# Layer one in pairs of chunks with 7 of 8 sub-products from the third pair, and an issue order reckoned at build time

## The chip, the cores and the metric

The kernel runs on one core of a Trainium2 chip. The metric is device time in microseconds (us). TensorE (PE) multiplies, VectorE (DVE), ScalarE (ACT) and GpSimd (POOL) work on tiles, and SyncE (SP) issues the DMAs. Every engine takes its own instructions in the order in which the program issued them.

## The reference

```python
def _attn_ref(q, k, v, centroids):            # B=2, H=8, S=768, D=64, 16 clusters
    ...
    mask = q_assign[:, :, :, None] == k_assign[:, :, None, :]
    scores = np.where(mask, scale * np.matmul(q, k.transpose(0, 1, 3, 2)), -1000000000.0)
    ...
    return np.matmul(attn, v)

def _moe_ref(x, w_in, w_out):                 # layer one: x 1536 x 512, w_in 512 x 2048 (float64)
    h = x @ w_in
    g = np.where(h > 0.0, h, np.exp(np.minimum(h, 0.0)) - 1.0)
    return g @ w_out

def _moe2_ref(x, domain_probs, w1, w2):       # layer two: 4 experts, 512 -> 1024 -> 512
    p = domain_probs / (domain_probs.sum(-1, keepdims=True) + 1e-09)
    for e in range(4):
        h = np.maximum(x @ w1[e], 0.0)
        out += p[:, e:e + 1] * (h @ w2[e])
    return out
```

## The kernel before

Attention (lines 100 to 587) runs first and leaves its output transposed in `xT`: three blocks of 512 tokens, each value as a high part and a low part, which together hold it to more bits than one float32r operand. A product of two split operands takes three matmuls: high by high, high by low, low by high. The change leaves the order of attention as it is.

Layer one cuts the 2048 hidden features into 16 chunks of 128. `emit_G1` (L783) forms one chunk for one block of 512 tokens: 4 slices of the features times 3 matmuls of 128x512, 12 in all, into one of two PSUM tiles `h`. The ELU follows: ACT takes Relu and Exp (L798, L799), DVE combines them with the PSUM value (L800), POOL splits the result into `gh` and `gl` (L801, L802). `emit_G2` (L968) multiplies with the chunk's rows of w_out: 4 outputs of 3 matmuls (L989). The chunks are taken in groups of 2, 4, 5 and 5 (`SIZES`, L598), a group being run for the first block, then the second, then the third; the four outputs stay in PSUM over all chunks of the group and are then copied to (L1012, ACT) or added to (L1014, DVE) the accumulators `acc`.

The weights of layer one arrive as float64. `w_split` (L716) converts a chunk from the 64-bit pattern in passes of 128x1024: ACT (L735), DVE (L737, L740, L743), ACT (L741, L747), DVE (L749), then ACT makes the high part (L751) and POOL the low part (L754). The first two chunks are converted during attention.

Layer two takes 16 pairs of chunks (256 features). A pair's first product is a 2 by 2 block product with 7 sub-products in place of 8 (`product`, L806, 6 matmuls each): for tokens 0 to 1023 with 512 columns (42 matmuls), for the last 512 tokens with 256 columns (42 matmuls). It needs sums of the operands: of the weights `w2_split` (L680, DVE), of x `x2_first`, `x2_second`, `x2_last` (L895 to L964). `quad_early` (L816) and `quad_late` (L838) issue the sub-products; three times TensorE goes on adding to a PSUM tile after ACT has copied it away:

```python
product(px, A11, "B11", s, True, True)
act.activation(out=m1, in_=px, func=AF.Copy)
product(pz, S1, "T1", s, True, True)
product(px, S2, "T2", s, False, True)
act.activation(out=u2, in_=px, func=AF.Copy)
```

The second product has 12 outputs of 6 matmuls (L989), which DVE scales by the expert's share and adds to `acc` (L1003).

The order is fixed at build time by hand: `tick` (L1060) and `advance` (L1056) move the weight and x generators on by one step at a time between the matmul steps, at positions given by `start` and `load_at` (L1041 to L1053). SP issues a chunk's two loads (`w_load`, L644) in that order too.

Of the kernel before, what the change touches and what calls it, by code (L numbers as in the profile page):

```python
# [46 lines left out]
def kernel(  # L47
# [37 lines left out]
    xT = [[xp.tile([128, 2, 512], F32R, tag=f"x{tb}{kk}", name="xT") for kk in range(KD)] for tb in range(NB)]  # L85
# [14 lines left out]
    def attention():  # L100
# [379 lines left out]
        def do_XS(w, i):  # L480
            j, r, hi, lo, cs = x_rows(w)
            if r == 0:
                return
            b, hp = divmod(j, HP)
            tb, o = divmod(b * S + cs.start, 512)
            hi, lo = (xT[tb][hp][:, i, o:o + XW] for i in range(2))
            pool.tensor_scalar(hi, xs_t[j][:, cs], 1.0, 0.0, ALU.mult, ALU.add)
            pool.tensor_tensor(lo, xs_t[j][:, cs], hi.bitcast(F32), ALU.subtract)  # L488
# [10 lines left out]
        def weights(n):  # L499

            for i in range(2):
                raw = cv_p.tile([128, 512, 2], I32, tag="raw", name="w_raw")
                w_load(n, [raw], i)
                yield
                yield
                tmp = cv_p.tile([128, 2, 512], I32, tag="tmp", name="w_tmp")
                yield from w_split(n, [tmp[:, x] for x in range(2)], i)
# [81 lines left out]

    SIZES = [2, 4, 5, DFF // 128 - 11]  # L598
    NSLOT = 9
    groups, chunks, steps = [], [], []  # L600
    at = 0
    for i, n in enumerate(SIZES):
        for tb in range(NB):
            for c in range(n):
                steps.append((1, tb, len(chunks) + c, c == 0, c == n - 1, i == 0, i == len(SIZES) - 1))
        for c in range(n):
            chunks.append((1, at + c))
        at += n
    NC1 = len(chunks)
    NP = E * F2 // 256  # L610
    BLOCKS = ((0, 8), (8, 4))
    for i in range(NP):
        for blk in range(len(BLOCKS)):
            steps.append((2, blk, NC1 + i, True, True, i == 0, i == NP - 1))
        chunks.append((2, i))
    NS = len(steps)

    last = [f"{t}{n % NSLOT}" for n in range(NC1 - SIZES[-1], NC1) for t in "hl"]
    early = [f"{t}{n % NSLOT}" for n in range(NC1, NC1 + NSLOT - SIZES[-1]) for t in "hl"]
    W2_TAGS = (early[:3] + early[4:6], last[1:4] + last[5:7])  # L620
    B22_TAG, G_TAG = early[3], last[4]
    A11, A12, A22, S1, S2, S3, S4 = range(7)

    X2_TAGS = (
        dict(zip(
            (A11, A12, S1, S2, S3, A22, S4),
            (("qh", "ql"), ("kl", "x00"), ("x01", "x02"), ("x03", "x10"), ("x11", "x12"), ("x13", early[6]),
             (early[7], last[0])),
        )),
        [f"x2{kk}" for kk in range(KD)] + last[7:],  # L630
    )
    W0 = 2
    LAG = 2
    moe_p = {}
    st_t, w_t = {}, {}

    def home(tag, shape, name, dt=F32R):
        p = xp if tag[0] == "x" else gen if tag[0] in "qk" else w01 if tag[1] in "01" else moe_p["w"]
        return p.tile(shape, dt, tag=tag, name=name)

    def w_tiles(n):
        return [home(f"{t}{n % NSLOT}", [128, 2, 512], f"w{t}{n % NSLOT}") for t in "hl"]

    def w_load(n, raw=None, half=None):  # L644
        ly, f = chunks[n]
# [4 lines left out]
        if ly == 1:  # L650
            for i, a in enumerate(raw):
                if half == 1 or i == 1:
                    src = w_out.bitcast(I32)[f * 128:(f + 1) * 128, :]
                    sp.dma_start(out=a.rearrange("p f t -> p (f t)"), in_=src)
                else:
                    src = w_in.bitcast(I32)[:, f * 256:(f + 1) * 256].rearrange("(k p) f -> p k f", p=128)
# [3 lines left out]
        else:  # L660
            e, f = divmod(f, F2 // 256)
# [9 lines left out]
    def split(h, l, x, eng):  # L671

        act.activation(out=h, in_=x, func=AF.Copy)
        yield
# [4 lines left out]

    def w2_split(n):  # L680

# [5 lines left out]
        t = gen.tile([128, 4, 2, 128], F32, tag="kh", name="T")  # L687
        dve.tensor_tensor(out=t[:, 0], in0=b12, in1=b11, op=ALU.subtract)
        dve.tensor_tensor(out=t[:, 2], in0=b22, in1=b12, op=ALU.subtract)
        yield  # L690
        dve.tensor_tensor(out=t[:, 1], in0=t[:, 0], in1=b22, op=ALU.subtract)
        dve.tensor_tensor(out=t[:, 3], in0=t[:, 1], in1=b21, op=ALU.add)
        yield
        ops = {}
        for x, names in (
            (a[:, :, 0], ("B11", "B21")), (t[:, 0:2].rearrange("p a k f -> p (a k) f"), ("T1", "T2")),
# [7 lines left out]
            else:  # L704
                o = home(tags[len(ops) // 2], [128, 2, m, 128], "w1op")
            yield from split(o[:, 0], o[:, 1], x, dve)
            for i, nm in enumerate(names):
                ops[nm] = [[o[:, z, 2 * i + kk] for kk in range(2)] for z in range(2)]
            yield
        h, l = (home(tag, [128, 2, 512], "w2op") for tag in tags[3:])  # L710
        b = b.rearrange("p (c d) -> p c d", c=2)
        yield from split(h, l, b, dve)
        w_t[n] = ops, (h, l)
        yield

    def w_split(n, tmp=None, half=None):  # L716
        if chunks[n][0] == 2:
            yield from w2_split(n)
            return
        a = st_t.pop(n)  # L720
        if n not in w_t:
            w_t[n] = w_tiles(n)
        h, l = w_t[n]
        if half is not None:
            h, l = h[:, half], l[:, half]

        small = tmp is not None
        a32, sg = tmp if small else [gtile(("qh", "kl", "kh")[n % 3], "wa", [128, 2, 512], I32), gtile("ql", "wsg", [128, 2, 512], I32)]  # L730
        at = (slice(None),) * (len(a.shape) - 1)
        hi, lo = a[at + (1,)], a[at + (0,)]
        x, sg = a32.bitcast(F32), sg.bitcast(F32)

        act.activation(out=x, in_=hi.bitcast(F32), func=AF.Abs)  # L735
        yield
        dve.tensor_scalar(x, x, LOW, TOP, ALU.max, ALU.min)  # L737
        if small:
            yield
        dve.tensor_scalar(a32, a32, 3, 0x40000000, ALU.logical_shift_left, ALU.bitwise_xor)  # L740
        act.activation(out=sg, in_=hi.bitcast(F32), func=AF.Sign)  # L741
        yield
        dve.scalar_tensor_tensor(  # L743
            out=a32, in0=lo, scalar=29, in1=a32, op0=ALU.logical_shift_right, op1=ALU.bitwise_or
        )
        yield
        act.activation(out=x, in_=x, func=AF.Abs)  # L747
        yield
        dve.tensor_tensor(out=x, in0=x, in1=sg, op=ALU.mult)  # L749
        yield  # L750
        act.activation(out=h, in_=x, func=AF.Copy)  # L751
        if small:
            yield
        pool.tensor_tensor(l, x, h.bitcast(F32), ALU.subtract)  # L754
        yield

    def moe():
# [8 lines left out]
        g_t, x2, x2_gen, w_gen2 = {}, [{}, {}], [[], []], {}  # L766
        turn = [0, 0]

# [14 lines left out]
        def emit_G1(s):  # L783
            ly, tb, n = steps[s][:3]
            if ly == 2:
                return
            wh, wl = w_t[n]
            ps = ps_h.tile([128, 512], F32, tag=f"h{s % 2}", name="h")
            for kk in range(KD):
                f = slice(kk * 128, (kk + 1) * 128)  # L790
                xh, xl = xT[tb][kk][:, 0], xT[tb][kk][:, 1]
                for i, (w, x) in enumerate(((wh, xh), (wh, xl), (wl, xh))):
                    pe.matmul(  # L793
                        ps, lhsT=w[:, 0, f], rhs=x, start=(kk == 0 and i == 0), stop=(kk == KD - 1 and i == 2)
                    )
            gh, gl = g_pair(1)
            r, gg = (scratch([128, 512], nm) for nm in ("r", "gg"))
            act.activation(out=r, in_=ps, func=AF.Relu, scale=-1.0)  # L798
            act.activation(out=r, in_=r, func=AF.Exp, scale=-1.0)  # L799
            dve.scalar_tensor_tensor(out=gg, in0=r, scalar=-1.0, in1=ps, op0=ALU.add, op1=ALU.max)  # L800
            pool.tensor_scalar(gh, gg, 1.0, 0.0, ALU.mult, ALU.add)  # L801
            pool.tensor_tensor(gl, gg, gh.bitcast(F32), ALU.subtract)  # L802
            g_t[s] = [(gh, gl)]


        def product(ps, a, b, s, start, stop):  # L806
            blk, n = steps[s][1:3]
            x, w = x2[blk][a], w_t[n][0][b]
# [7 lines left out]
        def quad_early(s):  # L816
            big = steps[s][1] == 0
# [4 lines left out]
            else:  # L822
                m1, u2, u3, c11 = (x[:, i] for x in (scratch([128, 2, n], "u"), scratch([128, 2, n], "u")) for i in range(2))
                c = scratch([128, 2, n], "c")
                c1, c2 = c[:, 0], c[:, 1]
            product(px, A11, "B11", s, True, True)
            act.activation(out=m1, in_=px, func=AF.Copy)  # L827
            product(pz, S1, "T1", s, True, True)
            product(px, S2, "T2", s, False, True)
            act.activation(out=u2, in_=px, func=AF.Copy)  # L830
            product(py, A12, "B21", s, True, True)
            dve.tensor_tensor(out=c11, in0=py, in1=m1, op=ALU.add)
            product(px, S3, "T3", s, False, True)
            act.activation(out=u3, in_=px, func=AF.Copy)
# [237 lines left out]
        def run_all(it):  # L1072
            for _ in it:
                pass
# [100 lines left out]
```

## Time and profile before

| | us |
|---|---|
| runs | 1036.28, 1039.0, 1037.94; median 1037.94 |
| profiled execution | 1037.14, of which the span 1035.3 |
| PE busy | 1016.5 (98% of the span), 5593 matmuls |
| DVE / ACT / POOL busy | 721.0 (70%) / 517.9 (50%) / 392.4 (38%) |

The span goes from the first to the last instruction of one profiled execution; what lies around it makes up the rest of its time. Matmuls overlap, so the pitch of a matmul is read from the chain of waits, where a run of matmuls stands with its time, and not from its own duration.

### The profile page before, as it was taken

Reading aid. Unit: us, or ns where it says so; the run is one execution under the profiler, and the core shown is the slowest. Engines: PE = TensorE matmul, PEld = TensorE weight load, DVE = VectorE, ACT = ScalarE, POOL = GpSimd, SP = SyncE. Lnnn points to the kernel's source line nnn. Section 1 sums busy time; section 2 is a strip of 40 time slices with the busy share of each in tenths; the row PEclk is TensorE's granted clock in tenths of the full one; section 3 lists DMA queues with packets and bytes.
Section 4 is the critical chain, followed back from the end, with each engine's and each line's share of the span. In section 5 each row is a group of like instructions: output and inputs, shape, how many; then the busy total and the mean of one; then the engine's idle time right before and its main releaser. Section 6 shows DMA issues by size and latency. Waiting matters only on the chain.

```text
span 1035.3 us, 14919 instructions
## 1 busy us (share of the span) xinstructions
PE 1016.5 (98%) x5593; PEld 881.6 (85%) x5593; DVE 721.0 (70%) x1151; ACT 517.9 (50%) x1002; POOL 392.4 (38%) x391
## 2 busy tenths in 40 slices
PE   8999999999999999999999999999999999999998
PEld 7989999989877888888887888888888888888887
DVE  7999999898679675233475766665776665776665
ACT  4989999888777554333345232332232323232321
POOL 4888888989688767344452000000000000000000
PEclk9999999999999999999999999999999999999999
DMA  6746654430333222000102101111101111101003
GB/s 157 188 110 157 145 136 111 118 91 3 125 120 123 82 82 82 1 0 1 41 1 82 40 3 41 41 41 41 41 1 41 42 41 41 41 1 41 1 1 122
DMA packets 61463, 66.65 MB, mean 64 GB/s; under 512 B 28944, under 2 KB 47376, under 8 KB 61392
## 3 DMA queue, kind: packets, MB, share of 16 engines
q1 hardware_dynamic: 61392, 65.71, 22.4%
q8 instruction: 44, 0.72, 0.3%
q14 instruction: 27, 0.22, 0.1%
HBM read 43.08 MB, written 3.15 MB: 45 GB/s over the span
## 4 chain that ended last, share of the span: by engine, by line
PE 80%; DVE 8%; POOL 4%; ACT 4%; issue 2%; DMA 1%; SPq 0%; DVEq 0%; POOLq 0%; ACTq 0%
PE a L989 35%; PE h L811 23%; PE h L793 11%; PE x L456 4%; PE tps L423 3%; PE s L375 2%; PE s L378 2%; POOL p L411 2%; DVE pl L444 1%; DVE nm L384 1%; DVE wa L743 1%; PE qkps L199 1%; DVE wa L737 1%; PE lps L244 1%; POOL xT L488 1%
## 5 line engine op out<-in xcount | busy, mean ns | idle before, releaser
L811 PE MATMUL h<-x,w1op 128*128 128x512 f32 (+1 forms) x1344 | 245.0, 337 | 2.2 <-ACT u L827 1.4
L811 PEld LDWEIGHTS h<-x,w1op 128*128 128x128 f32 x1344 | 211.7, 189 | 32.1 <-ACT u L827 1.6
L989 PE MATMUL a<-w2op,gh 128*128 128x512 f32 x768 | 237.2, 390 | 0.0
L989 PEld LDWEIGHTS a<-w2op,gh 128*128 128x128 f32 x768 | 142.1, 188 | 28.6 <-ACT acc L999 0.3
L1003 DVE SCALAR_TENSOR_TENSOR acc<-a,prob,acc 128x512 f32<-128x512 f32 x180 | 134.5, 748 | 34.2 <-PE a L989 34.1
L989 PE MATMUL a<-w2op,gl 128*128 128x512 f32 x384 | 149.6, 390 | 0.0
L793 PE MATMUL h<-xT,wh 128*128 128x512 f32 x384 | 118.6, 390 | 0.6 <-DVE gg L800 0.6
L800 DVE SCALAR_TENSOR_TENSOR gg<-r,h 128x512 f32<-128x512 f32 x48 | 32.9, 685 | 104.2 <-ACT r L799 83.0
L411 POOL TENSOR_SCALAR p<-e,sm 128x768 f32<-128x768 f32 x96 | 89.2, 936 | 34.4 <-DVE sm L405 24.4
L384 DVE TENSOR_REDUCE nm<-s 128x1 f32<-128x768 f32 x96 | 90.9, 947 | 2.8 <-PE s L378 2.6
L393 ACT ACTIVATE e<-s,nm 128x768 f32<-128x768 f32 x96 | 86.6, 902 | 4.3 <-POOL p L411 3.3
L423 PE MATMUL tps<-ident,p 128*128 128x128 f32 x576 | 83.7, 277 | 3.3 <-DVE pl L444 3.1
L793 PEld LDWEIGHTS h<-xT,wh 128*128 128x128 f32 x384 | 71.9, 188 | 16.3 <-DVE gg L800 1.4
L989 PEld LDWEIGHTS a<-w2op,gl 128*128 128x128 f32 x384 | 72.1, 188 | 15.2
L444 DVE TENSOR_TENSOR pl<-tps,ph 128x512 fp32r<-128x512 f32 x112 | 76.2, 684 | 6.6 <-ACT ph L436 5.0
L798 ACT ACTIVATE r<-h 128x512 f32<-128x512 f32 x48 | 28.6, 596 | 100.4 <-PE h L793 100.4
L801 POOL TENSOR_SCALAR gh<-gg 128x512 fp32r<-128x512 f32 x48 | 42.9, 894 | 94.5 <-DVE gg L800 92.6
L456 PE MATMUL x<-ph,v 128*128 128x256 f32 x288 | 76.4, 297 | 0.1
L989 PE MATMUL a<-gh,wh 128*128 128x512 f32 x192 | 74.9, 390 | 1.0 <-ACT acc L1012 0.9
L989 PE MATMUL a<-gl,wh 128*128 128x512 f32 x192 | 74.7, 389 | 0.0
L793 PE MATMUL h<-xT,wl 128*128 128x512 f32 x192 | 74.7, 389 | 0.0
L989 PE MATMUL a<-gh,wl 128*128 128x512 f32 x192 | 74.7, 389 | 0.0
(163 smaller groups left out, 1855.6 us busy)
## 6 DMA issues: line engine op xcount, KB each, us to landing
st<-in_moe_w_dram SPq DMA_DIRECT2D x32, 512.0 KB, 4.3
st<-in_moe_w_in_dram SPq DMA_DIRECT2D x14, 512.0 KB, 3.8
st<-in_moe_w_out_dram SPq DMA_DIRECT2D x14, 512.0 KB, 4.6
QA<-qh SPq DMA_DIRECT2D x30, 192.0 KB, 3.9
nq<-in_q_dram SPq DMA_DIRECT2D x16, 192.0 KB, 3.7
nk<-in_k_dram SPq DMA_DIRECT2D x16, 192.0 KB, 3.8
nv<-in_v_dram SPq DMA_DIRECT2D x8, 384.0 KB, 4.3
QB<-ql SPq DMA_DIRECT2D x16, 192.0 KB, 3.9
```

What stands on the lines that cost most here:

```text
L384: dve.tensor_reduce(out=m_t[w][:, i:i + 1], in_=s_t[HALF * w + i][:, :, 0:384], axis=AX.XY, op=ALU.max, negate=True)
L393: act.activation(out=e, in_=s_t.pop(u)[:, :, 0:384], func=AF.Exp, bias=m_t[w][:, i:i + 1], accum_out=e_t[w][0][:, i:i + 1])
L411: pool.tensor_scalar(p, e_t[w][1 + i].rearrange("p a b -> p (a b)"), e_t[w][0][:, i:i + 1], 1.0, ALU.mult, ALU.mult)
L423: pe.transpose(ps[:, x, :], p_t[w][i][:, c * 128:(c + 1) * 128], ident)
L444: dve.tensor_tensor(out=l, in0=ps, in1=h.bitcast(F32), op=ALU.subtract)
L456: pe.matmul(x_t[w], lhsT=v2[j][:, r, c, :], rhs=t[:, :, c, :], start=(c == 0 and t is ph[w]), stop=(c == T - 1 and t is pl[w]),)
L793: pe.matmul(ps, lhsT=w[:, 0, f], rhs=x, start=(kk == 0 and i == 0), stop=(kk == KD - 1 and i == 2))
L800: dve.scalar_tensor_tensor(out=gg, in0=r, scalar=-1.0, in1=ps, op0=ALU.add, op1=ALU.max)
L801: pool.tensor_scalar(gh, gg, 1.0, 0.0, ALU.mult, ALU.add)
L811: pe.matmul(ps, lhsT=w[wz][kk], rhs=x[xz][:, kk], start=(start and kk + i == 0), stop=(stop and kk == 1 and i == 2), skip_group_check=True,)
L989: pe.matmul(ps, lhsT=x, rhs=y, start=(opens and i == 0), stop=(closes and i == len(ops) - 1))
L1003: dve.scalar_tensor_tensor(out=t, in0=ps, scalar=pr, in1=t, op0=ALU.mult, op1=ALU.add)
```

## The change

Layer one is taken in 8 pairs of chunks. Each pair is run for the first block (a), the second (b) and the third (c). From the third pair on (`NPLAIN = 2`), blocks a and b are formed together by `quad_one`, the same 7 sub-products as in layer two with the ELU behind them; block c keeps `emit_G1`. For this the sums of x are made once (`x1_ops`) and those of the weights for each pair (in `w_pair`). The second product closes its PSUM tiles after each pair (`emit_G2_one`, 6 matmuls for an output). In layer two the first pair uses 8 plain sub-products (`plain_two`); the sums of x come after it (`x2_ops`). The high part of an activation moves from POOL to ACT, and low parts and sums go to DVE or POOL, whichever ends earlier by the reckoned clocks.

The order of the vector work is no longer written out. While the program is built, a clock for each engine is advanced by an assumed price of each instruction, with one more clock (`port`) for work that DVE and POOL can't do at the same time. Work of the weights and sums stands in `back`; `fill` issues it ahead of an instruction of the matmul path if it would end no later than that instruction could start, plus a tolerance. The loads of domain_probs move from the thirteenth step of layer one to its start.

```diff
-    SIZES = [2, 4, 5, DFF // 128 - 11]
-    NSLOT = 9
...
+    NC1 = DFF // 128
+    NP1 = NC1 // 2
+    NPLAIN = 2
+    END, LEAD = 4, 4
+    TIGHT, TOL, LOOSE = 0.0, 0.5, 0.7
...
+    clk, port = {act: 1.0, dve: 1.6, pool: 1.0, pe: 0.0}, [0.0]
+    COST = {act: (0.11, 0.00083), dve: (0.07, 0.00105), pool: (0.2, 0.0021)}
+    LATE, MM, MM2, BIAS = 0.16, 0.227, 0.53, 0.0
...
+    def ends(e, n, ready, lock):
+        if e is None:
+            return min(ends(dve, n, ready, lock) + BIAS, ends(pool, n, ready, lock))
+        return max(clk[e], ready, port[0] if lock else 0.0) + COST[e][0] + COST[e][1] * n
...
+    def w_pair(p):
...
+        yield from both(*(w_convert(n) for n in two))
+        yield from until("G1", p - 2)
+        yield from both(*(w_split(n, 0) for n in two))
...
+            for o, x, y, f in (
+                (b11, b12, b11, ALU.subtract), (b12, b22, b12, ALU.subtract), (b22, b11, b22, ALU.subtract),
+                (b21, b22, b21, ALU.add),
+            ):
+                t = yield None, 256, t, True
+                chosen[0].tensor_tensor(o, x, y, f)
+            yield from until("quad", p - 2)
+            yield from until("x1", min(2, p - NPLAIN + 1))
...
+        yield from until("G2", p - 2)
+        yield from both(*(w_split(n, 1) for n in two))
...
+        def fill(until):
+            for b in list(back):
+                while b in back and (b[1] is None or ends(*b[1]) <= until):
+                    if not step(b):
+                        break
+
+        def fg(e, n, ready, lock=False, tol=TOL):
+            fill(ready + tol)
+            return book(e, n, ready, lock)
...
+        def elu(c, r, t):
+            t = fg(act, 512, t)
+            act.activation(out=r, in_=c, func=AF.Relu, scale=-1.0)
+            t = fg(act, 512, t - LATE)
+            act.activation(out=r, in_=r, func=AF.Exp, scale=-1.0)
+            t = fg(dve, 512, t)
+            dve.scalar_tensor_tensor(out=r, in0=r, scalar=-1.0, in1=c, op0=ALU.add, op1=ALU.max)
+            return r, t
...
+        def quad_one(p, x, w, it):
...
+            product(px, x[A11], w["B11"], True, True)
+            t1 = copy(m1, px, 512, mm(6, max(tw, *(h_free.get(i, 0) for i in range(3)))))
+            product(pz, x[S1], w["T1"], True, True)
+            mm(6, 0)
+            product(px, x[S2], w["T2"], False, True)
+            t2 = copy(u2, px, 512, mm(6, t1))
+            product(py, x[A12], w["B21"], True, True)
+            t11 = add(c11, py, m1, 512, mm(6, 0))
+            product(px, x[S3], w["T3"], False, True)
+            t3 = copy(u3, px, 512, mm(6, t2))
+            t12 = add(c2, pz, u3, 512, t3)
+            next(it)
+            h0a = elu(c11, m1, t11)
+            product(px, x[A22], w["T4"], False, True)
+            t4 = mm(6, t3)
+            h1b = g_split(elu(c2, u3, t12))
+            next(it)
+            product(pz, x[S4], w["B22"], False, True)
...
+        def copy(o, ps, n, t):
+            t = fg(act, n, t, tol=TIGHT)
+            act.activation(out=o, in_=ps, func=AF.Copy)
+            return t
...
+            if p == NPLAIN:
+                while x1_gen in back:
+                    step(x1_gen)
+            it = emit_G2_one(p - 1, 2, g_t.get("c"))
+            if p < NPLAIN:
+                for k, tb in (("a", 0), ("b", 1)):
+                    g_t[k] = [emit_G1(tb, 2 * p + c) for c in range(2)]
...
+            else:
+                quad_one(p, x1, w_t["p", p], it)
...
+            if s == 0:
+                order = (4, 5, 6, 7, 0, 1, 2, 3)
+                emit_G2(s, order[:LEAD])
+                q = plain_two(s + 1)
+                next(q)
+                emit_G2(s, order[LEAD:])
+                run_all(q)
```

From the third pair on the matmul order of a pair is: the 7 sub-products with two outputs of block c of the pair before between the last three, the other two of these outputs, the third block's first product, then the second product of b and of a.

## Rows read from the trace of the kernel before

**Rows 1.** Windows: us, busy PE, PEld, DVE, ACT, POOL (counts), clock, DMA share, GB/s.
```profile
267.77:541.66 273.89, 272.28 (x1196) 223.65 (x1195) 160.99 (x170) 136.58 (x187) 165.85 (x118) 1.00 0.16 54
541.66:592.03 50.37, 48.19 (x248) 40.71 (x247) 34.67 (x55) 21.95 (x41) 5.77 (x4) 1.00 0.13 42
592.03:623.03 31.00, 31.00 (x157) 26.49 (x157) 20.33 (x34) 9.58 (x18) 0.00 (x0) 1.00 0.10 35
```

**Rows 2.** Chain that ended last: start, time, engine, tile, line, instructions.
```profile
387.78 2.72 PE a L989 x12
...
606.99 3.68 PE h L811 x30
623.03 6.80 PE h L811 x30
```

**Rows 3.** TensorE's timeline: gaps in layer one's start and the change of layers.
```profile
299.85 0.50 PE L989 MATMUL a<-gh,wh 128*128 128x512 f32 x1 [0.93 <-ACT acc L1012]
...
555.85 2.43 PE L811 MATMUL h<-x,w1op 128*128 128x256 f32 x18 [1.43 <-ACT u L827]
558.81 1.69 PE L811 MATMUL h<-x,w1op 128*128 128x256 f32 x12 [0.53 <-ACT u L834]
```

**Rows 4.** Groups by line and shape from 330 us on: busy us, mean ns.
```profile
L800 DVE SCALAR_TENSOR_TENSOR gg<-r,h 128x512 f32<-128x512 f32 x37 | 25.4, 686 | 92.4 <-ACT r L799 75.4 <-issue 16.9
...
L676 DVE TENSOR_TENSOR w1op<-T,w1op 128x512 fp32r<-128x512 f32 x32 | 21.7, 682 | 0.0
L798 ACT ACTIVATE r<-h 128x512 f32<-128x512 f32 x36 | 21.5, 597 | 97.6 <-PE h L793 97.6
L1014 DVE TENSOR_TENSOR acc<-a,acc 128x512 f32<-128x512 f32 x32 | 19.8, 680 | 0.0
...
L735 ACT ACTIVATE wa<-st 128x1024 f32<-128x1024 f32 x7 | 7.9, 1126 | 0.0
L688 DVE TENSOR_TENSOR T<-st 128x256 f32<-128x256 f32 x16 | 7.8, 486 | 0.0
...
L912 DVE TENSOR_TENSOR st<-acc 128x1024 f32<-128x1024 f32 x1 | 1.2, 1217 | 0.0
```

**Rows 5.** Timelines of DVE and POOL: conversion steps and a subtraction without a delay.
```profile
272.63 0.69 DVE L737 TENSOR_SCALAR wa<-wa 128x1024 f32<-128x1024 f32 x1
...
280.70 0.69 DVE L740 TENSOR_SCALAR wa<-wa 128x1024 int32<-128x1024 int32 x1
...
281.92 1.22 DVE L743 SCALAR_TENSOR_TENSOR wa<-st,wa 128x1024 int32<-128x1024 int32 x1
...
306.02 1.22 DVE L749 TENSOR_TENSOR wa<-wa,wsg 128x1024 f32<-128x1024 f32 x1
...
434.24 1.29 POOL L802 TENSOR_TENSOR gl<-gg,gh 128x512 fp32r<-128x512 f32 x1
```

**Rows 6.** Timelines of POOL and DVE where the two overlap.
```profile
290.69 2.77 POOL L754 TENSOR_TENSOR wl<-wa,wh 128x1024 fp32r<-128x1024 f32 x1
...
291.23 3.31 DVE L743 SCALAR_TENSOR_TENSOR wa<-st,wa 128x1024 int32<-128x1024 int32 x1
...
329.18 3.40 POOL L754 TENSOR_TENSOR wl<-wa,wh 128x1024 fp32r<-128x1024 f32 x1
...
330.82 2.47 DVE L1014 TENSOR_TENSOR acc<-a,acc 128x512 f32<-128x512 f32 x4
```

**Rows 7.** ACT's timeline: the copies within one 7-product block of layer two.
```profile
624.49 0.60 ACT L827 ACTIVATE m<-h 128x512 f32<-128x512 f32 x1 [4.56 <-PE h L811]
627.15 0.60 ACT L830 ACTIVATE u<-h 128x512 f32<-128x512 f32 x1 [2.06 <-PE h L811]
629.93 0.60 ACT L834 ACTIVATE u<-h 128x512 f32<-128x512 f32 x1 [2.18 <-PE h L811]
```

**Rows 8.** SP's timeline: the loads of domain_probs.
```profile
331.33 0.91 SPq L1026 DMA_DIRECT2D prob<-in_moe_domain_probs_dram  x2
```

More of the change, by code (lines that the diff above doesn't have):

```diff
@@ L506, in weights @@
                 tmp = cv_p.tile([128, 2, 512], I32, tag="tmp", name="w_tmp")
-                yield from w_split(n, [tmp[:, x] for x in range(2)], i)
+                g = w_convert(n, [tmp[:, x] for x in range(2)], i)
+                next(g)
+                for _ in g:
+                    yield
         w_gen = [g for n in range(W0) for g in (weights(n),)]
@@ L611 @@
+    END, LEAD = 4, 4
+    TIGHT, TOL, LOOSE = 0.0, 0.5, 0.7
+    W0 = 2
     BLOCKS = ((0, 8), (8, 4))
[L612 to L615, printed above, removed]
+    steps = [(blk, NC1 + i, i == 0, i == NP - 1) for i in range(NP) for blk in range(len(BLOCKS))]
     NS = len(steps)
-    last = [f"{t}{n % NSLOT}" for n in range(NC1 - SIZES[-1], NC1) for t in "hl"]
-    early = [f"{t}{n % NSLOT}" for n in range(NC1, NC1 + NSLOT - SIZES[-1]) for t in "hl"]
@@ L620 @@
[L620 to L630, printed above, removed]
-    )
[L632 to L635, printed above, removed]
+    A11, A12, A22, S1, S2, S3, S4, A21 = range(8)
@@ L637, in home, with until @@
+    def until(what, p):
+        while told[what] < p:
+            yield
     def home(tag, shape, name, dt=F32R):
-        p = xp if tag[0] == "x" else gen if tag[0] in "qk" else w01 if tag[1] in "01" else moe_p["w"]
+        p = xp if tag[0] == "x" else gen if tag[0] in "qk" else w01 if tag in ("i0", "i1", "o0", "o1") else moe_p["w"]
         return p.tile(shape, dt, tag=tag, name=name)
-    def w_tiles(n):
-        return [home(f"{t}{n % NSLOT}", [128, 2, 512], f"w{t}{n % NSLOT}") for t in "hl"]
@@ new lines, in w_split, with both @@
+    def w_split(n, part):
+        x, t = w_x[n]
+        w_t.setdefault(n, {})[part] = w = home(f"{'io'[part]}{n % 4}", [128, 2, 512], "w")
+        t = yield act, 512, max(t, w_free["io"[part], n % 4]), False
+        act.activation(out=w[:, 0], in_=x[:, part], func=AF.Copy)
+        t = yield None, 512, t, True
+        lows(w[:, 1], x[:, part], w[:, 0], chosen[0])
+        w_rdy[n, part] = t
+    def both(a, b):
+        g = [[a, next(a)], [b, next(b)]]
+        while g:
+            k = min(range(len(g)), key=lambda k: 0 if g[k][1] is None else ends(*g[k][1]))
+            t = yield g[k][1]
+            try:
+                g[k][1] = g[k][0].send(t)
+            except StopIteration:
+                g.pop(k)
@@ new lines, in piece, with sums @@
+        def piece(o, x, names, t0):
+            u = yield act, 128 * x.shape[1], t0, False
+            act.activation(out=o[:, 0], in_=x, func=AF.Copy)
+            u = yield None, 128 * x.shape[1], u, True
+            lows(o[:, 1], x, o[:, 0], chosen[0])
+            for nm in names:
+                w_rdy[n, nm] = u
+        def sums():
+            u = w_rdy["ld", n]
+            for o, x, y, f in (
+                (0, b12, b11, ALU.subtract), (1, t[:, 0], b22, ALU.subtract), (2, b22, b12, ALU.subtract),
+                (3, t[:, 1], b21, ALU.add),
+            ):
+                u = yield None, 256, u, True
+                chosen[0].tensor_tensor(t[:, o], x, y, f)
+                if o == 1:
+                    yield from piece(*parts[1], u)
+            yield from piece(*parts[2], u)
@@ new lines, in plain @@
+        def plain():
+            yield from piece(*parts[0], w_rdy["ld", n])
+            yield from piece(*parts[3], w_rdy["ld", n])
+        if k == 0:
+            yield from both(piece(*parts[0], w_rdy["ld", n]), piece(*parts[1], w_rdy["ld", n]))
+        else:
+            yield from both(plain(), sums())
+        if k < 2:
+            yield from until("G2", NP1 - 2 + k)
+        else:
+            yield from until("G22", k - 2)
+        w_t[n][1] = h, l = [home(tag, [128, 2, 512], "w2op") for tag in tags[3:]]
@@ L765, in moe, with run_all, advance, step @@
         ps_a = P("ps_a", 5, space=PSUM)
-        g_t, x2, x2_gen, w_gen2 = {}, [{}, {}], [[], []], {}
+        g_t, x1, x2, w_gen = {}, {}, [{}, {}], {}
         turn = [0, 0]
+        acc, going = {}, []
+        g_free, h_free, a_free, g_rdy, g_slot, x_rdy, acc_t = {}, {}, [0.0] * 5, {}, {}, {}, {}
+        def run_all(it):
+            for _ in it:
+                pass
+        def advance(k=1):
+            for _ in range(k):
+                going[:] = [it for it in going if next(it, 0) is None]
+        back = []
+        def step(b):
+            t = None if b[1] is None else book(*b[1])
+            try:
+                b[1] = b[0].send(t)
+            except StopIteration:
+                back.remove(b)
+                return False
+            return b[1] is not None
+        def begin(it):
+            back.append([it, None])
+            return back[-1]
+        def fill(until):
[6 more added lines that the diff above has]
+            return book(e, n, ready, lock)
+        def mm(k, ready):
+            clk[pe] = max(clk[pe], ready) + k * MM
+            return clk[pe] + 0.2
+        def must(what, p):
+            while told[what] < p:
+                for b in list(back):
+                    if step(b):
+                        break
         def scratch(shape, name):
@@ L797, in emit_G1 @@
[L797 to L808, printed above, removed]
+                        ps, lhsT=w[:, wz, f], rhs=x[:, xz, kk % 2], start=(kk == 0 and i == 0),
@@ L809, in product @@
+                        stop=(kk == KD - 1 and i == 2),
+                    )
+            t = mm(12, max(w_rdy.get((n, 0), 0), h_free.get(1 + n % 2, 0)))
+            if tb == 2:
+                w_free["i", n % 4] = t
+            r, t = elu(ps, scratch([128, 512], "r"), t)
+            h_free[1 + n % 2] = t
+            return r, t
+        def product(ps, x, w, start, stop):
             for kk in range(2):
@@ new lines, in copy, with add, term @@
+        def copy(o, ps, n, t):
+            t = fg(act, n, t, tol=TIGHT)
+            act.activation(out=o, in_=ps, func=AF.Copy)
+            return t
+        def add(o, ps, y, n, t):
+            t = fg(dve, n, t, tol=TIGHT)
+            dve.tensor_tensor(out=o, in0=ps, in1=y, op=ALU.add)
+            return t
+        def term(s, ps, i, nm, start, ready=0.0):
+            blk, n = steps[s][:2]
+            bring(s, i, nm)
+            product(ps, x2[blk][i], w_t[n][0][nm], start, True)
+            return mm(6 if blk == 0 else 6 * MM2, max(ready, x_rdy[blk, i], w_rdy[n, nm]))
@@ L818, in quad_early, with bring, quad_two @@
+        def bring(s, i, nm):
+            blk, n = steps[s][:2]
+            while (blk, i) not in x_rdy or (n, nm) not in w_rdy:
+                for b in list(back):
+                    if step(b):
+                        break
+        def quad_two(s):
+            big = steps[s][0] == 0
             n = 512 if big else 256
@@ L847, in quad_late, with relu, low @@
                 g_t[s] = [((h0,), (l0,)), ((h1,), (l1,))]
-            def low(l, h, x):
+                slots = [(turn[0] - 1 + i) % 5 for i in range(2)]
+                slots = slots[0], slots[1], slots[0], slots[1]
+            g_slot[s] = slots
+            def relu(h, x, n, t, k):
+                t = fg(act, n, max(t, g_free.get(slots[k], 0)), tol=TIGHT)
+                act.activation(out=h, in_=x, func=AF.Relu)
+                return t
+            def low(l, h, x, n, t):
+                t = fg(dve, n, t, tol=TIGHT)
                 dve.scalar_tensor_tensor(
@@ L883, in low @@
[L883 to L888 removed]
+                return t
+            r0a = relu(h0a, c11, n, t11, 0)
+            r1b = relu(h1b, c2, n, t12, 1) if big else 0
+            t4 = term(s, px, A22, "T4", False, t3)
+            t5 = term(s, pz, S4, "B22", False, t12)
@@ new lines, in moe, with chain @@
+        for b in range(B):
+            sp.dma_start(
+                out=prob[:, b * T:(b + 1) * T, :],
+                in_=domain_probs[b * S:(b + 1) * S, :].rearrange("(p t) e -> p t e", t=T),
+            )
+        def chain():
+            for p in range(1, NP1):
+                yield from w_pair(p)
+            for n in range(NC1, NC1 + NP):
+                yield from w2_split(n)
+                if n == NC1:
+                    yield from until("sA", 1)
+                else:
+                    if n == NC1 + 1:
+                        yield from until("sB", 1)
+                    for k in ((n + 1, n + 2) if n == NC1 + 1 else (n + 2,)):
+                        if k < NC1 + NP:
+                            w_load(k)
@@ L1139, in moe @@
+            emit_G2(s + 1, range(1 if s + 2 < NS else 0, 4))
+            told["G22"] = s // 2
             if s + 2 < NS:
-                run_all(late)
+                run_all(q)
             g_t.pop(s + 1)
```

754 lines of the change are left out of this document (425 added, 329 removed).

## The prediction

> **What bounds the kernel now.** I read the windows first, to see which stage leaves TensorE idle, then the chain of waits for the pitch of a matmul, then TensorE's timeline for its gaps, and last the prices on the other engines. Attention ends at 267.77 us and is not touched. From there on TensorE is busy for nearly all of every window, at a granted clock of 1.00, the 2.4 GHz level [rows 1]. The pitch is 2.72 / 12 = 0.2267 us for a 512-column matmul and 3.68 / 30 = 0.1227 us for a 256-column one [rows 2].
>
> With these the windows can be split into work and idle time. Layer one with the first 42 matmuls of layer two holds 1152 + 42 matmuls, 270.7 us, and takes 273.89: 3.2 us are lost. The stretch 541.66 to 592.03 holds 162 wide and 84 narrow ones, 36.7 + 10.3 = 47.0 us, and takes 50.37: 3.4 us are lost. After that a pair takes 31.00 us with TensorE busy for 31.00: nothing is lost [rows 1]. The gaps are eviction copies that come late in the first 50 us of layer one, and narrow products that wait for a copy of their own PSUM tile at the change of layers [rows 3]. So only two things can shorten the run: fewer matmuls, or these 6.6 us.
>
> **The change part by part.** *Products in layer one.* Pairs 2 to 7 form tokens 0 to 1023 with 7 sub-products of 6 matmuls, 42, where 48 stood; the third block stays at 24 and the second projection at 72. That is 6 x 6 x 0.2267 = 8.16 us less. *First pair of layer two*: 8 sub-products for 7, 6 wide and 6 narrow matmuls more, 1.36 + 0.74 = 2.10 us. Net -6.06 us, all on the path. Bounds: the products are the same instructions on the same shapes as L811 and L793, so I take the pitch as it is.
>
> *Evictions.* Partial sums are closed after each pair instead of after 2, 4, 5 and 5 chunks: 96 evictions for 48. They are hidden: four outputs take TensorE 5.4 us and DVE 2.47 us [rows 2, 6]. If five PSUM tiles were full, one more would cost 0.68 us [rows 4].
>
> *Vector work of a pair from the third on*, against 138 x 0.2267 = 31.3 us of TensorE. DVE, if it did all: 2 chunks converted at 0.69 + 0.69 + 1.22 + 1.22, 7.6 us [rows 5]; 12 low parts (4 of weights, 2 of their sums, 6 of activations) at 0.68, 8.2; 4 sums of 256 at 0.49, 1.9; 6 ELU steps at 0.69, 4.1; 3 additions and 12 evictions at 0.68, 10.2. Sum 32.0 us, over the 31.3. The planner can give low parts and sums to POOL at 1.29 us each [rows 5]. ACT: 12 ELU steps, 3 copies and 12 high parts at 0.60, 16.2, and 6 conversion passes at 1.13, 6.8: 23.0 us, 73% [rows 4].
>
> *What POOL can take.* The rows show that the two engines exclude each other: L743 takes 1.22 us alone, but 3.31 us when it starts during a POOL subtraction that ends at 293.46 [rows 5, 6]; four evictions that read PSUM run in 2.47 us under a POOL subtraction, undisturbed [rows 6]. So POOL gains only while DVE reads PSUM, here some 12.2 us of a pair (3 ELU steps, 3 additions, 12 evictions), about 9 POOL instructions, 6 us of DVE's work. That leaves 26 of 31.3 us on DVE, 82%: the pair fits, with waits. The Trainium skill, page "SBUF — State Buffer", section "Who interferes with whom", states the same as an exclusive lock, and adds that a DVE instruction with two SBUF inputs takes part in it. By that, the ELU steps and low parts on c11, c2 and c1, which the planner books without the lock, would be held up by POOL too; the sum without any exclusion would be 21 of 31.3 us and no wait at all. The trace agrees on L743.
>
> *Order within a pair.* Each 7-product block has three hand-overs where TensorE needs an ACT copy of the tile it goes on with. In layer two such copies start 0.04 to 0.1 us after the product and take 0.60 us [rows 7], with 1.36 us of other matmuls over them: slack 0.7 us. A conversion pass of 1.13 us in front would cost up to 0.5 us; none in front, nothing. 18 hand-overs: 0 to 8 us. I take 0.1 each, 2 us, near the low end, since the build-time clocks let a background pass in only if it ends before the copy can start, and their rates for 512 columns (ACT 0.535, DVE 0.608, TensorE 0.227 us) lie within 0.08 us of the rows [rows 2, 4].
>
> *Start of layer one.* Pair 2 needs the sums of x and its converted weights 264 matmuls, 59.8 us, after 267.77. Until then DVE and POOL have: 4 conversions 15.3; 12 ELU steps 8.3; about 14 evictions on DVE 9.5; 11 low parts of activations 7.5, 8 of weights 5.4; 4 sums 1.9; 12 passes of 1024 over x at 1.22, 14.6. That is 62.5 us of DVE for 58, of which POOL may take 9 under the 17.8 us that read PSUM: 53 of 58. It just fits. Bounds 0 to 4.5 us (POOL helps nothing); I take 1.5 for this and the first two pairs, less than the 3.2 lost now, as evictions may now go to whichever of ACT and DVE is free.
>
> *Change of layers.* The first pair's plain products need no copy between two products, so the gaps of 1.43 and 0.53 us go; their operands have two outputs' time (10.9 us) for four passes of ACT and DVE. Next late are the sums S1 to S4 for the next pair. Bounds 0 to 3.4 us (as now); I take 1.0.
>
> *Moved at no cost.* The probability loads go from 331 us to the start; SP is then 0.91 us longer busy [rows 8], while the load behind them waits for chunk 2's conversion; uncovered it would be 0.9 us. In layer two weight splits may go to POOL; DVE has 31.00 - 20.33 = 10.7 us idle in a pair [rows 1], and a low part held up by 1.29 us stands before 5 us of other matmuls. Bounds -1 to +1 us; I take 0.
>
> **Sum.** 1037.14 us for the profiled execution, less 6.06, less the 6.6 lost now, plus 2 + 1.5 + 1.0 = 1029.0. The median of the runs, 1037.94, is 0.80 above that execution, so 1029.8 for a median.
>
> **The rivals.** *Nothing new is lost* (under 2 us): 1025.3 to 1027. For it: layer two runs without a gap. Against: ACT and DVE are twice as full in a layer-one pair.
>
> *DVE becomes the bound of layer one.* Each wait like that of L743 costs 2.1 us. If POOL saved DVE nothing, a pair would be 0.7 us over its matmuls; with one such wait each it is 2.8 us over. Over 6 pairs that is 4 to 17 us, with 4.5 at the start and 1 at the change of layers 9.7 to 22; middle 14 in place of 4.5: 1039, no change. By the lock rule of the Trainium skill above, applied to the steps booked without it, the time would come out this way. For it: 32.0 us of demand. Against: POOL had 166 of 274 us busy in layer one with TensorE at 272 [rows 1].
>
> *Slower: ACT stands in the hand-overs.* ACT takes its instructions in order. If the pass in front of a copy itself waits for a DVE step that POOL has delayed by 2.1 us, TensorE waits 2.1 - 0.7 = 1.4 us there. Without the 2 us taken for order the sum is 1027.8; so it decides from 10 of 18 hand-overs (14 us, 1041.8); all 18 give 25 us, 1053; taken 14, 1047. For it: one conversion alternates ACT and DVE four times. Against: the clocks resynchronise whenever ACT waits for TensorE.
>
> *The change does not do what it says*, for one because the products saved return as waits for the x sums in each block: the matmuls' 6.06 us are gone, idle time as taken: 1035.9, no change.
>
> **How the numbers follow.** About 0.3%, 3.1 us, can be told from no change here: faster is below 1034.8, slower above 1041.1. Chances: the forecast (1027 to 1034.8) 0.63, nothing new lost 0.14, DVE the bound 0.11, the slower case 0.08, the products' gain lost 0.04. Faster 0.77, same 0.15, slower 0.08. The range is 1024.5 (no loss at all, less a margin for the runs' spread) to 1040 (DVE the bound); it leaves out the slower case and the edges.
>
> **What would show it.** Right: 252 matmuls of the 7-product kind in layer one and 1356 of the 7- and 8-product kind in layer two, at 0.2267 and 0.1227 us, pair starts in layer one 31.3 to 31.8 us apart, TensorE gaps released by ACT copies of some tenths, POOL busy in both layers. Wrong: a gap of over 2 us ahead of the first 7-product block (x sums late), pair spacings above 33 us with DVE near 100% (DVE the bound), or gaps of over 1 us after most copies (hand-overs).

## The result, and the profile after

The changed kernel takes 1026.82 us (median; 1025.78 to 1029.96), the kernel before 1037.68 us in the same comparison: ratio 0.9901, 95% interval 0.9875 to 0.9926, faster by 1.0%. Forecast were 1029.8 us in a range of 1024.5 to 1040.

The profiled execution took 1025.78 us, its span 1024.0 for 1035.3. First the windows: layer one, the change of layers, and one later pair of layer two (columns as in [rows 1]).

```profile
267.12:520.43 253.31, 253.31 (x1117) 209.48 (x1117) 221.12 (x317) 174.01 (x266) 37.10 (x30) 1.00 0.17 59
520.43:580.11 59.68, 59.05 (x302) 50.20 (x301) 45.00 (x67) 30.39 (x51) 9.77 (x9) 1.00 0.15 54
580.11:611.12 31.01, 31.01 (x157) 26.50 (x157) 17.12 (x27) 9.47 (x18) 7.80 (x8) 1.00 0.10 35
```

Layer one holds 1116 matmuls, 253.0 us at 0.2267: 0.3 us are lost. The second window holds 210 wide and 90 narrow matmuls, 47.6 + 11.0 = 58.6 us: 1.0 us is lost. Layer two's later pairs take 440.1 us in all, 0.5 more than the same work took before. So 1.8 us are lost behind attention where some 6.4 were: the prediction's 6.6 counts from the first record of layer one (267.77), while the windows here count from the chain of waits, which has 267.93 there. With 6.06 us of matmuls gone, 4.6 us less lost and a start of layer one that is 0.8 us earlier in this execution (267.12 for 267.93), that is 11.5 us; the span fell by 11.3.

Now the six pairs with 7 sub-products, one window each (the first and the last):

```profile
327.31:358.60 31.29, 31.29 (x140) 25.93 (x139) 29.24 (x44) 22.73 (x34) 4.75 (x4) 1.00 0.20 68
...
483.71:514.99 31.28, 31.28 (x140) 25.91 (x139) 19.55 (x27) 16.20 (x25) 3.57 (x2) 1.00 0.00 1
```

Each of the six takes 31.27 to 31.29 us, its 138 matmuls (31.3 us). TensorE is never idle, though in the first four DVE is busy for 28 to 29 us of a pair, ACT for 22 to 23 and POOL for about 5. The last has no weights left to convert and asks for less. The two pairs ahead of them are fuller still, and there too TensorE has no gap:

```profile
267.12:327.31 60.19, 60.19 (x265) 49.48 (x265) 56.79 (x77) 49.20 (x74) 4.50 (x4) 1.00 0.21 71
```

The largest gap that is left stands in the change of layers. These are rows of TensorE's, DVE's and POOL's timelines:

```profile
549.84 5.75 PE L970 MATMUL h<-x,w1op 128*128 128x512 f32 x24 [0.49 <-DVE gl L1042]
```

```profile
547.91 1.28 DVE L655 TENSOR_TENSOR x<-st,x 128x512 fp32r<-128x512 f32 x1 [0.70 <-ACT x L1190]
549.11 0.68 DVE L1042 SCALAR_TENSOR_TENSOR gl<-h,gh 128x512 fp32r<-128x512 f32 x1
```

```profile
547.34 1.30 POOL L1220 TENSOR_TENSOR st<-acc,st 128x512 f32<-128x512 f32 x1 [25.93 <-DVE st L1220]
```

A POOL sum holds up a DVE subtraction (1.28 us for 0.68) until it ends at 548.64; the low part behind that subtraction comes late, and TensorE waits 0.49 us for it. This is the lock of [rows 6], as the page "SBUF — State Buffer" of the Trainium skill, section "Who interferes with whom", states it.

### The profile page after: what moved, and what is told of

Same layout as the page of the kernel before. It is cut to its first block, busy times and chain, and to the rows that moved or that the text cites. A ratio compares the mean times of both kernels' runs of the same rounds, so it can differ in the third digit from the quotient of the medians.

```text
span 1024.0 us, 15049 instructions
## 1 busy us (share of the span) xinstructions
PE 1008.4 (98%) x5569; PEld 877.4 (86%) x5569; DVE 749.1 (73%) x1221; ACT 560.5 (55%) x1088; POOL 362.9 (35%) x393
## 4 chain that ended last, share of the span: by engine, by line
PE 77%; DVE 1%; ACT 1%; issue 0%; POOL 0%; DMA 0%; SPq 0%; ACTq 0%; POOLq 0%
PE h L970 28%; PE a L1317 26%; PE a L1283 13%; PE h L956 6%; PE x L456 2%; PE tps L423 1%; PE s L378 1%; PE s L375 1%; POOL p L411 0%; DVE pl L444 0%; DMA KB<-ohT 0%; ACT e L393 0%; DVE x L655 0%; DVE nm L384 0%; DVE w_tmp L703 0%
## 5 line engine op out<-in xcount | busy, mean ns | idle before, releaser
L1283 PE MATMUL a<-gh,w 128*128 128x512 f32 x384 | 122.8, 389 | 0.0
L657 POOL TENSOR_TENSOR w2op<-st,w2op 128x1024 fp32r<-128x1024 f32 x14 | 33.6, 2403 | 237.4 <-ACT w2op L808 237.4
L1010 ACT ACTIVATE u<-h 128x256 f32<-128x256 f32 (+1 forms) x87 | 42.4, 487 | 100.8 <-PE h L970 98.9
L1283 PEld LDWEIGHTS a<-gh,w 128*128 128x128 f32 x384 | 72.1, 188 | 14.9
L1112 ACT ACTIVATE gh<-c 128x512 fp32r<-128x512 f32 x60 | 37.7, 630 | 72.3 <-PE a L1317 55.8
L1283 PE MATMUL a<-gl,w 128*128 128x512 f32 x192 | 74.7, 389 | 0.0
L456 PE MATMUL x<-pl,v 128*128 128x256 f32 x288 | 72.2, 283 | 0.1
L423 PEld LDWEIGHTS tps<-ident,p 128*128 128x128 f32 x576 | 64.8, 141 | 7.5 <-DVE pl L444 4.8
L436 ACT ACTIVATE ph<-tps 128x512 fp32r<-128x512 f32 x112 | 65.2, 600 | 6.7 <-PE tps L423 5.0
```

The costliest lines, as they stand in the source:

```text
L423: pe.transpose(ps[:, x, :], p_t[w][i][:, c * 128:(c + 1) * 128], ident)
L436: act.activation(out=t_out(ph[w], g), in_=ps, func=AF.Copy)
L456: pe.matmul(x_t[w], lhsT=v2[j][:, r, c, :], rhs=t[:, :, c, :], start=(c == 0 and t is ph[w]), stop=(c == T - 1 and t is pl[w]),)
L1283: pe.matmul(ps, lhsT=x, rhs=y, start=(i == 0), stop=(i == len(ops) - 1))
```

## The experiments

My theory: behind attention the time is the number of matmuls times their pitch, and the planned order keeps the rest off TensorE's path. Rivals: the gain is from the order alone; the 7-product pairs cost what they save; the margins of the order don't matter. Medians below stand beside 1037.96 to 1038.39 us for the kernel before, measured along with them.

### Undo the parts, one by one and together

**All pairs plain.**

```diff
-    NPLAIN = 2
+    NPLAIN = 8
```

with no sums of x, and the last pair's blocks in the order b, a.

> All eight pairs of layer one formed with plain products, no sums of x or of its weights; the rest of the change stays. Theory (TensorE's matmuls set the time, and the new order leaves almost no idle time, 1.8 us behind attention): 36 matmuls more at 0.2267 us are +8.2 us, so 1035.0 us, 0.9975 of the kernel before. Rival (the vector work of the 7-product pairs costs TensorE about as much as the matmuls save, and the gain is all from order): the same 1027 us or less, ratio 0.989.

Measured: 1038.22 us, ratio 1.0004 (0.9992 to 1.0015): 11.4 us slower than the changed kernel, 3.2 us more than the 8.2 of the theory. TensorE's timeline of this kernel shows where:

```profile
526.22 0.50 PE L1283 MATMUL a<-gl,w 128*128 128x512 f32 x1 [0.91 <-POOL gl L657]
...
562.43 3.93 PE L970 MATMUL h<-x,w1op 128*128 128x512 f32 x16 [1.24 <-DVE gl L1042]
```

My edit had formed a before b in the last pair but used b first, so the third block's activations waited for the buffers of a. The repair forms b first:

```diff
-                for k, tb in (("a", 0), ("b", 1)):
+                for k, tb in (("b", 1), ("a", 0)) if last else (("a", 0), ("b", 1)):
...
```

> As the all-plain kernel, but in its last pair block b is formed and split before a, so that the third block's activations do not wait for the slots of a, which only this edit had brought. Theory (of the 11.4 us that the all-plain kernel is slower, 8.2 are matmuls and the rest is this wait and one held-up step behind it): 1035 to 1036.5 us. Rival (the 7-product pairs save more than their matmuls): 1038.

Measured: 1035.58 us, ratio 0.9978 (0.9966 to 0.9990). The 7-product pairs are worth 8.8 us, of which 8.2 are matmuls; the 0.6 us between are inside the intervals. In this kernel's chain of waits a pair takes 32.64 us (361.25 to 393.89), in the changed kernel 31.28. That the 7-product pairs cost TensorE what they save is out.

**Layer two's first pair with 7 sub-products again.**

```diff
-        q = plain_two(0)
+        q = quad_two(0)
...
-                q = plain_two(s + 1)
+                q = quad_two(s + 1)
```

with the weights' sums for it, and without the splits of A21.

> Layer two's first pair with 7 sub-products again, the rest of the change stays. Theory (the plain products are there because the sums of x come late): 2.1 us of matmuls go, but TensorE waits for the sums S1, S3, S2, S4, which are a chain of passes after the last output of layer one; more than 2.1 us of new gaps between 525 and 560 us, time 1027 to 1032. Rival (the chain is hidden by the third block's outputs and the 8 plain sub-products are not needed): 1024.7 us, ratio 0.9875.

Measured: 1036.51 us, ratio 0.9987 (0.9976 to 0.9998): 9.7 us slower than the changed kernel with 2.1 us of matmuls less. This is beyond the 1027 to 1032 us that I had expected. TensorE's timeline, and a window over the stretch behind the gaps:

```profile
524.12 1.43 PE L965 MATMUL h<-x,w1op 128*128 128x512 f32 x5 [1.47 <-DVE x L655]
529.96 0.80 PE L965 MATMUL h<-x,w1op 128*128 128x512 f32 x1 [4.40 <-ACT x L1185]
531.21 6.84 PE L965 MATMUL h<-x,w1op 128*128 128x512 f32 x17 [0.46 <-DVE x L655]
```

```profile
531.20:538.00 6.80, 6.79 (x17) 5.12 (x17) 3.81 (x5) 2.36 (x4) 0.00 (x0) 0.57 0.01 2
```

The sums of x come one after the other, and TensorE waits for the low part of one (1.47 us), then for the high and the low part of the next (4.40 and 0.46 us). Behind these gaps 17 matmuls take 6.84 us, 0.40 each: the granted clock is 0.57, near the 1.2 GHz level, which costs another 3.0 us.

**Both edits**: the matmuls of the kernel before, in the new order. I ran it with the unrepaired and with the repaired last pair.

> The two edits together: the same number and shapes of matmuls as the kernel before, only the grouping in pairs and the order from build-time clocks are left of the change. Theory: idle time behind attention 2 to 7 us where the kernel before has 6.6 and the changed one 1.8, so 1033 to 1038 us, ratio 0.995 to 1.000; with the sum of the other two edits it should be near 1026.8 + 8.2 + (first-pair result - 1026.8). Rival (order is the whole gain): 1027 us, ratio 0.989.

> The same with layer two's first pair at 7 sub-products: the matmuls of the kernel before, in the order by pairs and clocks. Theory (forming all three blocks in the last pair leaves the sums of x uncovered, whatever the slots): 1035.5 + 10 = 1044 to 1048 us, slower than the kernel before. Rival (it was the wait for slots): 1038 or less.

Measured: 1049.08 us, ratio 1.0105 (1.0087 to 1.0123), and 1045.74 us, ratio 1.0070 (1.0053 to 1.0086). The theory for the first of them, 1033 to 1038 us, was wrong: with the matmuls of the kernel before, pairs and clocks make the kernel *slower*. With the repaired kernels the four corners are:

| us | first pair of layer two 7 | first pair 8 |
|---|---|---|
| layer one plain | 1045.74 | 1035.58 |
| layer one 7 of 8 from the third pair | 1036.51 | 1026.82 |

The 7 of 8 in layer one is worth 9.2 and 8.8 us, the plain first pair 10.2 and 9.7 us: the two hardly touch each other. Against the kernel before, pairs and clocks cost 8 us, and the other two parts bring 19. The order is not at fault in layer one: in the repaired all-plain kernel that takes 261.5 us (268.42 to 529.89) for 1152 matmuls of 261.2, where the kernel before lost some 3 us. What it costs stands at the change of layers, where the repaired kernel with both edits shows the waits of the kernel with 7 in the first pair again: 1.48, 4.40 and 0.46 us.

The reason is in the old grouping: there the last group of five chunks ran block after block. Two blocks go into the sums of x, and the later of them, b, was complete 14 us ahead of layer two's first product, while the third block still ran; the sums were made from 512.98 to 525.22 us. Rows of DVE's and TensorE's timelines in the kernel before:

```profile
509.45 2.48 DVE L1014 TENSOR_TENSOR acc<-a,acc 128x512 f32<-128x512 f32 x4
```

```profile
526.33 6.96 PE L811 MATMUL h<-x,w1op 128*128 128x512 f32 x30
```

In pairs the blocks are complete only in the last pair. With the first pair at 7 products again, the last output of a, here the later block, is added to `acc` up to 516.35 us, and layer two's first product starts at 520.90:

```profile
515.66 0.69 DVE L1293 TENSOR_TENSOR acc<-a,acc 128x512 f32<-128x512 f32 x1 [0.29 <-PE a L1278]
```

So in the changed kernel the sums of x have little more to hide behind than the 8 plain sub-products.

### How much room the start has

```diff
-    NPLAIN = 2
+    NPLAIN = 1
```

> 7 sub-products already in the second pair, seven pairs in place of six. Theory (the vector work before the first such pair fits in 58 us with 53, so with half the time it does not): 1.4 us of matmuls go, but the sums of x, 14.6 us of passes, have to be done 27 us after the start of layer one beside 2 conversions and the work of pair 0; a wait of 3 to 12 us ahead of the first 7-product block, time 1028 to 1037. Rival (there was room to spare): no gap, 1025.5 us, ratio 0.9885.

Measured: 1033.38 us, ratio 0.9952 (0.9938 to 0.9967): 6.6 us slower with 1.4 us of matmuls less. TensorE waits for a high part of the weights' sums in the first 7-product block, and the matmuls behind the wait are slow again (12 in 4.71 us, 0.39 each):

```profile
304.63 4.71 PE L970 MATMUL h<-x1s,wT 128*128 128x512 f32 x12 [5.35 <-ACT wT L836]
```

The start was full, as reckoned: DVE 56.8 of 60.2 us in the changed kernel.

### What the planner's knowledge is worth

**DVE alone**, POOL never chosen:

```diff
         if e is None:
-            return min(ends(dve, n, ready, lock) + BIAS, ends(pool, n, ready, lock))
+            e = dve
```

and the same in `book`.

> Every low part and sum that the planner could give to POOL goes to DVE. In the changed kernel a 7-product pair shows DVE 28 to 29 us busy and POOL 5 us in about 4 instructions of 31.3 us. Theory (POOL is a relief valve, not needed: 28.5 + 4 x 0.68 = 31.2 us of DVE just fit): pair spacing 31.3 to 31.6 us, time 1026 to 1029. Rival (DVE is the bound as soon as POOL is gone, 32.0 us by the prediction's sum and more by bunching): spacing 32 us and over, time 1031 to 1036.

Measured: 1026.46 us, ratio 0.9884 (0.9870 to 0.9898), no slower than the changed kernel. The window over the six pairs:

```profile
327.56:515.24 187.68, 187.68 (x829) 155.46 (x829) 165.97 (x260) 122.77 (x190) 0.00 (x0) 1.00 0.16 57
```

DVE does all in 166.0 us, and TensorE still has no gap. The last pair takes only 19.8 us of DVE; the five that still convert weights take 28.4 to 30.5 us of 31.28, the fullest being this one:

```profile
358.84:390.12 31.28, 31.28 (x139) 25.91 (x139) 30.47 (x52) 22.65 (x35) 0.00 (x0) 1.00 0.20 68
```

The 0.49 us gap of the change of layers is gone too. The difference of 0.36 us from the changed kernel is inside the intervals, so I don't call it better.

**A planner that doesn't know the lock:**

```diff
-        return max(clk[e], ready, port[0] if lock else 0.0) + COST[e][0] + COST[e][1] * n
+        return max(clk[e], ready) + COST[e][0] + COST[e][1] * n
```

> The build-time clocks no longer know that DVE and POOL exclude each other; the work is the same, more of it goes to POOL and the order differs. Theory (exclusion is real and the planner's knowledge of it is what keeps the ACT copies on time): DVE steps of 1.2 us show 2 to 3 us again, and TensorE waits at hand-overs, 3 to 12 us in all, time 1030 to 1039. Rival (there is slack enough for such waits): 1026 to 1028.

Measured: 1045.09 us, ratio 1.0078 (1.0058 to 1.0098), 18 us slower than the changed kernel and beyond what I expected. DVE's and POOL's timelines at the start:

```profile
291.42 2.90 DVE L698 TENSOR_SCALAR wa<-wa 128x1024 int32<-128x1024 int32 x1
...
297.22 3.06 DVE L711 TENSOR_TENSOR wa<-wa 128x1024 f32<-128x1024 f32 x1
```

```profile
291.35 2.42 POOL L657 TENSOR_TENSOR x1s<-xs,x1s 128x1024 fp32r<-128x1024 f32 x1 [8.72 <-ACT x1s L1159]
296.79 2.41 POOL L1149 TENSOR_TENSOR xs<-xs 128x1024 f32<-128x1024 f32 x1 [3.03 <-DVE xs L1149]
```

Steps of 0.69 and 1.22 us take 2.90 and 3.06 behind POOL. But it is not the hand-overs within the pairs that pay, as I had thought: the pairs stay 31.28 us apart. The losses stand in the two crowded places. From the start of layer one to the first 7-product block this kernel takes 69.2 us (269.82 to 338.99, by the first records) for 60.2; TensorE waits there 6.0 us for ELU steps of DVE. The rest is in the change of layers. What the ignorance changes is above all how much goes to POOL: in that first stretch it gets eight steps of weights and sums, 18.6 us, where the changed kernel gives it one of 0.74 us. Beside the experiment with DVE alone this says that the knowledge is worth 18 us only to a planner that may choose POOL at all; what the lock and what POOL's longer steps have in it was not tried apart.

**A planner that lets background work in early:**

```diff
-    TIGHT, TOL, LOOSE = 0.0, 0.5, 0.7
+    TIGHT, TOL, LOOSE = 3.0, 3.0, 3.0
```

> Background work may be issued ahead of a matmul path instruction if it would end up to 3 us after that could start, in place of 0, 0.5 and 0.7 us; the work is the same. Theory (slow rival of the prediction, made to happen: ACT passes of 1.13 us stand in front of the copies, slack 0.7 us): up to 2 passes in front of each of 18 hand-overs cost 0.5 to 1.5 us, TensorE gaps released by ACT copies of 9 to 27 us in all, time 1036 to 1054. Rival (the tolerances hardly matter): 1027.

Measured: 1082.03 us, ratio 1.0422 (1.0403 to 1.0440), far beyond the 1036 to 1054 us that I expected. The same work in another order costs 55 us. TensorE's timeline shows whom it waits for:

```profile
347.67 1.65 PE L970 MATMUL h<-x1s,wT 128*128 128x512 f32 x6 [2.25 <-ACT m L1010]
375.54 0.50 PE L1283 MATMUL a<-gh,w 128*128 128x512 f32 x1 [3.10 <-DVE acc L1298]
```

There are waits for ACT's copies, as forecast, but in layer one's pairs (330 to 525 us) they are 2.5 us, while waits for evictions are 13.4 us: conversion steps stand in front of the evictions on DVE (L711 from 371.00 and from 372.47, the evictions from 374.81 on) until TensorE has no free PSUM tile. In layer two (from 600 us on) ACT's copies cost another 7.7 us.

**The unbooked steps booked** with the lock (the ELU and low parts of c11, c2, c1):

```diff
-            h0a = elu(c11, m1, t11)
+            h0a = elu(c11, m1, t11, True)
...
```

> The DVE steps with both inputs in SBUF (ELU of c11, c2, c1 and their low parts in layer two) are booked with the exclusion. Theory (in layer one's pairs TensorE has no idle time left, so it can only help at the change of layers and in layer two, where 1.5 us are lost): 1025.5 to 1027.5. Rival (the unbooked steps hold up something that matters): 1024.5 or less, or over 1028.

Measured: 1026.68 us, ratio 0.9891 (0.9876 to 0.9906): no difference, as the theory said.

### DVE's margin

Layer one's tiles closed after each chunk, 192 evictions for 96:

```diff
-                pe.matmul(ps, lhsT=x, rhs=y, start=(i == 0), stop=(i == len(ops) - 1))
...
+                    ps = ps_a.tile([128, 512], F32, tag="a", name="a")
...
+                    ops = [(w[:, 0, col], gh), (w[:, 0, col], gl), (w[:, 1, col], gh)]
+                    for i, (x, y) in enumerate(ops):
+                        pe.matmul(ps, lhsT=x, rhs=y, start=(i == 0), stop=(i == len(ops) - 1))
+                    t = mm(3, max(a_free.pop(0), t, w_rdy.get((2 * p + c, 1), 0)))
...
```

> Layer one's second product closes its PSUM tiles after each chunk: 192 evictions in place of 96, the matmuls unchanged. It adds 12 x 0.60 to 0.68 us of DVE to a pair that has 28.5 us in 31.3, so 36 us. Theory (DVE has some 3 us left in a pair and is the next bound): pairs 34 to 37 us apart, time 1045 to 1062. Rival (POOL takes up what DVE cannot, as it is nearly idle): pairs below 32 us, 1027 to 1031.

Measured: 1093.45 us, ratio 1.0519 (1.0495 to 1.0542), worse than both ends of what I expected. The pairs stand 41 us apart (422.15 to 463.36), though DVE is busy for only 35.6 us of that pair, and for 85% of the stretch around it:

```profile
330.00:560.00 230.00, 194.57 (x754) 147.91 (x754) 195.96 (x302) 117.99 (x183) 19.51 (x15) 0.90 0.14 46
```

```profile
460.19 1.35 PE L970 MATMUL h<-xT,w 128*128 128x512 f32 x4 [3.81 <-DVE w L655]
...
463.36 5.12 PE L970 MATMUL h<-x1s,wT 128*128 128x512 f32 x12 [1.81 <-ACT wT L836]
```

TensorE waits for the next pair's weights, 3.81 us for a low part of DVE's and 1.81 us for a high part of ACT's, and then runs 12 matmuls in 5.12 us, 0.43 each. So a pair that overruns DVE (35.6 us for 31.3) loses more than the overrun: 9.9 us.

## Why the prediction was right

*Matmuls.* The net of -6.06 us stands. Pairs stand 31.28 us apart, for 32.64 in the repaired all-plain kernel: the 1.36 us between are 6 matmuls of 0.2267.

*Hand-overs in the pairs.* Taken at 2 us, measured 0: in the windows above TensorE's busy time equals the window. My reason held (a pass is let in only if it ends before the copy can start), the term was too large. The rival with ACT in the hand-overs, at 0.08, did not happen; with the loose tolerances, which were to make it happen, TensorE waited in layer one's pairs mostly for late evictions on DVE, a mechanism that I had not named.

*Start of layer one.* Taken at 1.5 us, measured at most 0.3. "It just fits" was right: with half the time it cost 8 us beside the matmuls.

*Change of layers.* Taken at 1.0 us, measured 1.0, but the step behind it was wrong. I booked the plain first pair as 2.10 us of cost that removes the gaps of [rows 3], some 2 us. In fact it is worth 9.7 us, because in pairs the later of the two blocks is complete 4.6 us ahead of layer two's first product, where it was 14.4. I had the late sums only "for the next pair". That my sum came out here is luck: the change holds both the harm and its cure, and I had priced neither of them so.

*DVE as the bound.* 32.0 us a pair was too high: durations of 0.68 us overlap by some 0.08 with the next instruction's, as the four evictions in 2.47 us of [rows 6] show, and DVE alone needs 28.4 to 30.5 in the pairs that convert weights. So POOL's part, on which I had let the pair's fit depend, is not needed; without it the time is the same. The lock does reach the ELU steps booked without it: at 430.17 and 431.00 two of them take 0.92 and 1.22 us for 0.68 beside POOL's sums of the weights, but TensorE waits for neither.

*The size.* The forecast change was 8.1 us, the measured one 10.9. The 2.8 us between are about the 2.7 us of idle time booked and not there (4.5 for 1.8).

What stays open: why layer one started 0.8 us earlier was not tried. Its first record stands between 267.0 and 270.5 us in the single traces of the kernels here, which all have the same order of attention, so differences of a few us between single executions say little. Nor were the parts of the new order tried apart (grouping, clocks, high parts on ACT, loads at the start).

## What to carry to other kernels

Where one engine has no slack, a cut in its work pays in full only if the order keeps every other engine's work out of its way; test the order with the same work in a worse one, which here cost up to 55 us. When a regrouping makes results complete later, look for what was prepared meanwhile: an algorithm with more arithmetic and no preparation can be the cheaper one there for a single step. In a sum of an engine's load, use the pitch of instructions in a row and not their durations.

## What was not expected of the hardware

A gap in TensorE's work can be paid twice. After waits of 1.47, 4.40 and 0.46 us between 523 and 531 us, the granted clock was 0.57, near the 1.2 GHz level, over the next 6.8 us and a 512-column matmul took 0.40 us for 0.2267; with 0.93 or 1.43 us of waiting, as in [rows 3], the window's clock stayed at 1.00. The Trainium skill, page "TensorE: Matmul & The Clock Gate", section "What's actually happening", names these two clock levels and has the idle one as the default; the trace agrees on the two levels. And a DVE step on one SBUF tile with two scalars (L698, 0.69 us alone) is held up by POOL as a step with two tiles is: 2.90 us. The Trainium skill, page "SBUF — State Buffer", section "Who interferes with whom", counts such steps among those that can contend; the trace agrees.
